# Fused attention, feed-forward and expert kernel: first pass of the first block cut after four slices, routing tables moved behind the weights, scheduler durations rewritten, load buffers pooled

## Chip, cores, metric

The kernel runs on one core of one Trainium2 chip. The metric is device time in microseconds (us) of one execution; lower is better.

## The reference

Three layers follow each other, on 3072 tokens of 384 features.

```python
for t in range(S):                                   # linear attention, 4 batches x 8 heads, head size 48
    cur = einsum('bhd,bhe->bhde', u * k[t], v[t])
    y[t] = einsum('bhd,bhde->bhe', r[t], state + cur)
    state = w * state + einsum('bhd,bhe->bhde', k[t], v[t])
h = x @ w_in                                         # 384 -> 2048
g = where(h >= 1, h, where(h <= -1, 0, (h + 1) ** 2 / 4))
x = g @ w_out                                        # 2048 -> 384
expert = argmax(normalised(x) @ normalised(emb).T / tau)   # 8 experts
out = gate * (maximum(x @ w1[expert], 0) @ w2[expert])     # 384 -> 1024 -> 384
```

All inputs are float32. The kernel keeps that precision by splitting each operand into a high and a low part and by adding three matrix products for each one of the reference (`prod3`, lines 201 to 204).

## The kernel before

**Attention** is cut into 24 units of 128 tokens. A unit loads two tiles (`att`, line 235, and `attn`, line 231). DVE scales r and k (`prep_rk`, L341); POOL makes `kk`, `ru` and `dv` (L347, L353, L355, L375) with a reduction on DVE between (`dg`, L360); PE multiplies k and r (`s0_pe`, L382); DVE masks the product (L390); PE makes the unit's output from `dv`, the carried state and the masked product (`s1_pe`, L399 to L413) and the unit's addition to the state (`s2_pe`, L422), which DVE adds and ACT decays (L433, L441). ACT and DVE split the output into `xh` and `xl` (L446, L453), which are the input of the first feed-forward layer.

**The first feed-forward layer** works on six blocks of 512 tokens, that is four units each, and on 16 slices of 128 hidden features. One slice of one block is a group of nine matrix products into `psh` (`m1_h`), a chain ACT, ACT, ACT, DVE, ACT, POOL that makes `gh` and `gl` (L529, L533, L536, L539, L543, L548), and nine products into three accumulators `acc` (`m1_out`). The weights arrive in 16 chunks, each for two slices, in turn of `w_in` and `w_out`. They are stored as 64-bit words; each chunk is one ACT, four DVE, one ACT and one POOL instruction (`w_abs`, L252; `w_bits`, L260, L262, L265, L268; `w_hi`, L283; `w_lo`, L287).

There is one set of accumulators, and so blocks can only alternate by storing a partial sum (`m1_evac`, L571 and L573, then L583 to DRAM) and by adding it later (L576). The first two blocks do that: `steps` (built from `HF`) runs slices 0 to 7 of block 0, 0 to 7 of block 1, 8 to 15 of block 0 and 8 to 15 of block 1. Blocks 2 to 5 then run their 16 slices each. The expert layer follows, with seven blocks.

**The order of the work** is made by `Schedule`, a planner in the kernel that runs at build time: every piece of work is a task with an engine, a duration, dependencies, buffers and a due time. It takes, of the tasks that can start earliest, the one due first, and the instructions are issued in that order. So each engine's queue, and SP's queue of DMAs, is fixed by the table of durations and due times. The list `T` holds the due time of each slice; `TB[m]` is the first of block m, from which the units' due times follow. Where the planner sees PE idle before the first slice, the program fills in `keep_warm` products on an unused accumulator (L460).

The routing tables (`tables3`, `tables4`, `tables5`: the normalised expert embedding and a check of w) are sixteen short DVE instructions and a few others, needed first by `pick_e0`, after the second pass of block 0. Load buffers are two for `att` and two for weight chunks (`w64`).

Of the kernel before, what the change touches and what calls it, by code (L numbers as in the profile page):

```python
# [138 lines left out]
def d_dve(n):  # L139
    return n / 960 + 0.066  # L140
# [14 lines left out]
def d_pe(n):  # L155
    return n / 2400 + 0.002
# [3 lines left out]
def fused_kernel(ctx, tc, att, wcol, wrow, ub, ucol, win, wout, emb, tau, w1, w2, out):  # L160
# [68 lines left out]
    def att_load(u, part):  # L229
# [4 lines left out]
        if part != "v":  # L234
            att_t[u] = atp.tile([128, O_K], F32, tag="att", name="att", bufs=2)
# [658 lines left out]
    for u in range(NU):  # L894
# [5 lines left out]
        ab.tag = "attb"  # L900
# [8 lines left out]
        rk = add("DVE", d_dve(1024), lambda u=u: prep_rk(u), [l0], due - 8, use=[ab])  # L909
        kk = add("Pool", d_pool(384), lambda u=u: prep_kk(u), [l2, wkc], due - 6, alloc=[kkb], use=[nb])  # L910
        ru0 = add("Pool", d_pool(384), lambda u=u: prep_ru(u, 0), [l2, ubl], due - 10, alloc=[rub], use=[nb])
        ru1 = add("Pool", d_pool(384), lambda u=u: prep_ru(u, 1), [ru0], due - 9.5, use=[nb, rub])
        dg = add("DVE", d_dve(384), lambda u=u: prep_dg(u), [ru1], due - 4.5, alloc=[dgb], use=[rub])
        dv = add("Pool", d_pool(384), lambda u=u: prep_dv(u), [dg, l1], due - 4.5, alloc=[dvb], use=[ab, dgb])
        s0 = add("PE", 1.15, lambda u=u: s0_pe(u), [rk], due - 7, alloc=[a0, a1], use=[ab])
        e0 = add("DVE", d_dve(512), lambda u=u: s0_ev(u, 0), [s0], due - 9, alloc=[atb], use=[a0])
        e1 = add("DVE", d_dve(512), lambda u=u: s0_ev(u, 1), [s0, e0], due - 9, use=[a1, atb])
        c = u % UPB
        s1 = add("PE", 2.0 if c else 1.35, lambda u=u: (xt_tiles(unit_blk[u][0]), s1_pe(u)),
# [7 lines left out]
        lo_of[u] = add("DVE", d_dve(384), lambda u=u: s3_lo(u), [s3h], due, use=[yb] + list(xbuf[m]))  # L927
        u_tasks += [lo_of[u], s1, dv, kk]
        if c != UPB - 1:
# [5 lines left out]
            p = add("DVE", 2 * d_dve(192) + 0.1, lambda u=u: s2_ev(u), [s2, s2e.get(u - 1 if c else u - 2)],  # L935
# [8 lines left out]
    for ci, c in enumerate([x for f in range(NF // 2) for x in (("in", f), ("out", f))]):  # L944
# [17 lines left out]
    for k, s in enumerate(steps):  # L962
# [6 lines left out]
        r = add("ACT", d_act(n), lambda k=k, n=n: got.update({("a", k): m1_relu(got["h", k], n)}), [h], T[k], alloc=[ab], use=[hb])  # L969
        q = add("ACT", d_act(n), lambda k=k: m1_over(got["a", k]), [r], T[k], use=[ab])  # L970
        q = add("ACT", d_act(n), lambda k=k: m1_sq(got["a", k]), [q], T[k], use=[ab])
# [373 lines left out]
```

## Time and profile before

| | |
|---|---|
| median of 3 runs | 779.70 us (778.98 to 780.13) |
| the profiled execution's own time | 779.42 us |
| its span, first to last instruction | 777.6 us |
| PE busy in the span | 745.2 us (96%) |
| DVE busy | 342.4 us (44%) |
| ACT busy | 397.4 us (51%) |
| POOL busy | 305.9 us (39%) |
| mean granted TensorE clock | 0.983 |

The span leaves 1.8 us of the execution outside. Shares over the whole span mix two stages: the first sixth, in which attention, weight chunks and slices compete, and the rest. How to read the rows below: a timeline row gives the start, the duration and the instruction, with the idle time before it in brackets; a group row gives count, busy time, mean duration in ns and idle time. A matrix product's shown duration is longer than its distance to the next one, since products are pipelined; distances are read from the starts.

### The profile page before, as it was taken

The numbers are of one execution on the slowest core, as the hardware profiler recorded it, in microseconds if no ns is written. First come the engines' busy times: TensorE is split into PE (matmuls) and PEld (weight loads), VectorE is DVE, ScalarE is ACT, GpSimd is POOL, SyncE is SP. The second block draws the span as 40 slices with busy tenths as digits, with TensorE's granted clock in tenths as the row PEclk, the third lists the DMA queues.
The fourth block names the chain that finished last, engine by engine and source line by source line (L and its number), as shares of the span: only waits on it lengthen the run. The fifth ranks groups of instructions, "written<-read, shape, count | busy, mean of one in ns | idle before, by whom it ended". The sixth has DMA issues, their size and how long they took to land.

```text
span 777.6 us, 12491 instructions
## 1 busy us (share of the span) xinstructions
PE 745.2 (96%) x5070; PEld 614.0 (79%) x5070; DVE 342.4 (44%) x584; ACT 397.4 (51%) x696; POOL 305.9 (39%) x258
## 2 busy tenths in 40 slices
PE   8878886999999999999999999999999999999996
PEld 7756665778777877887777878888798888888995
DVE  6999997721454135311452132522323333232442
ACT  3345476676346655664556645877532424242442
POOL 6877999543465255623654232333210101010000
PEclk9989989999999999999999999999999999999999
DMA  7655364210522014101212011410211111101100
GB/s 281 199 194 179 142 202 140 80 46 0 201 87 73 1 40 148 58 36 58 85 56 80 0 40 42 145 60 1 80 31 52 40 42 41 41 20 41 62 21 26
DMA packets 22277, 61.67 MB, mean 79 GB/s; under 512 B 1977, under 2 KB 7746, under 8 KB 22210
## 3 DMA queue, kind: packets, MB, share of 16 engines
q1 hardware_dynamic: 22210, 60.78, 23.0%
q8 instruction: 42, 0.69, 0.4%
q14 instruction: 25, 0.20, 0.1%
HBM read 49.76 MB, written 11.01 MB: 78 GB/s over the span
## 4 chain that ended last, share of the span: by engine, by line
PE 83%; DVE 11%; POOL 3%; issue 2%; ACT 1%; POOLq 0%; ACTq 0%; DVEq 0%
PE psh L202 13%; PE psh L203 12%; PE psh L204 12%; PE acc L202 8%; PE acc L204 8%; PE acc L203 8%; PE o L204 4%; PE o L202 4%; PE o L203 4%; PE psa L382 2%; DVE sc L265 2%; DVE sc L260 2%; DVE sc L262 1%; DVE att L341 1%; DVE at L390 1%
## 5 line engine op out<-in xcount | busy, mean ns | idle before, releaser
L548 POOL TENSOR_TENSOR gl<-a,gh 128x512 fp32r<-128x512 f32 x96 | 128.5, 1338 | 189.9 <-ACT gh L543 185.0
L539 DVE TENSOR_TENSOR a<-psh,a 128x512 f32<-128x512 f32 x96 | 66.1, 688 | 187.2 <-ACT a L536 186.9
L202 PE MATMUL psh<-xh,win_h 128*128 128x512 f32 x288 | 117.9, 409 | 8.3 <-DVE a L539 8.3
L203 PE MATMUL psh<-xl,win_h 128*128 128x512 f32 x288 | 115.8, 402 | 3.6 <-DVE xl L453 3.6
L202 PE MATMUL acc<-gh,wout_h 128*128 128x512 f32 x288 | 117.2, 407 | 2.0 <-ACT gh L543 2.0
L203 PE MATMUL acc<-gl,wout_h 128*128 128x512 f32 x288 | 115.0, 399 | 3.6 <-POOL gl L548 3.6
L529 ACT ACTIVATE a<-psh,half 128x512 f32<-128x512 f32 x96 | 65.8, 685 | 99.1 <-PE psh L204 95.8
L204 PE MATMUL psh<-xh,win_l 128*128 128x512 f32 x288 | 115.7, 402 | 0.0
L204 PE MATMUL acc<-gh,wout_l 128*128 128x512 f32 x288 | 114.7, 398 | 0.0
L543 ACT ACTIVATE gh<-a 128x512 fp32r<-128x512 f32 x96 | 60.5, 630 | 72.3 <-DVE a L539 72.1
L683 POOL TENSOR_TENSOR sq<-sq 128x512 f32<-128x512 f32 (+1 forms) x14 | 15.9, 1134 | 182.9 <-ACT sq L678 149.6
L806 ACT ACTIVATE gh<-psh 128x512 fp32r<-128x512 f32 (+1 forms) x56 | 29.9, 535 | 105.0 <-PE psh L204 98.6
L811 DVE SCALAR_TENSOR_TENSOR gl<-psh,gh 128x512 fp32r<-128x512 f32 (+1 forms) x56 | 34.3, 612 | 102.1 <-ACT gh L806 102.1
L202 PEld LDWEIGHTS psh<-xh,win_h 128*128 128x128 f32 x288 | 54.9, 190 | 24.6 <-DVE a L539 10.2
L202 PEld LDWEIGHTS acc<-gh,wout_h 128*128 128x128 f32 x288 | 54.6, 189 | 18.2 <-ACT gh L543 2.9
L203 PEld LDWEIGHTS acc<-gl,wout_h 128*128 128x128 f32 x288 | 54.7, 190 | 16.7 <-POOL gl L548 4.8
L203 PEld LDWEIGHTS psh<-xl,win_h 128*128 128x128 f32 x288 | 55.2, 192 | 16.0 <-DVE xl L453 3.9
L204 PEld LDWEIGHTS psh<-xh,win_l 128*128 128x128 f32 x288 | 55.2, 192 | 13.2
L204 PEld LDWEIGHTS acc<-gh,wout_l 128*128 128x128 f32 x288 | 54.6, 190 | 13.0
L204 PE MATMUL o<-w2h,gl 128*128 128x384 f32 x192 | 64.7, 337 | 0.0
L202 PE MATMUL o<-w2h,gh 128*128 128x384 f32 x192 | 64.7, 337 | 0.0
L203 PE MATMUL o<-w2l,gh 128*128 128x384 f32 x192 | 64.5, 336 | 0.0
(155 smaller groups left out, 1324.5 us busy)
## 6 DMA issues: line engine op xcount, KB each, us to landing
att<-att SPq DMA_DIRECT2D x22, 736.0 KB, 4.5
attn<-att SPq DMA_DIRECT2D x24, 384.0 KB, 4.2
w<-win SPq DMA_DIRECT2D x8, 768.0 KB, 4.8
w<-wout SPq DMA_DIRECT2D x8, 768.0 KB, 4.5
x1d<-x SPq DMA_DIRECT2D x6, 768.0 KB, 3.7
out<-o SPq DMA_DIRECT2D x11, 384.0 KB, 2.5
x1f<-x1d SPq DMA_DIRECT2D x5, 768.0 KB, 4.9
hw<-w SPq DMA_DIRECT2D x8, 384.0 KB, 3.8
```

The lines of the kernel that those rows point to most:

```text
L202: nc.tensor.matmul(o, lhsT=sh, rhs=mh, start=first, stop=False, skip_group_check=True)
L203: nc.tensor.matmul(o, lhsT=sh, rhs=ml, start=False, stop=False, skip_group_check=True)
L204: nc.tensor.matmul(o, lhsT=sl, rhs=mh, start=False, stop=last, skip_group_check=True)
L260: nc.vector.tensor_scalar(out=m, in0=m, scalar1=2.0 ** -15, scalar2=None, op0=ALU.max)
L265: nc.vector.scalar_tensor_tensor(out=tu, in0=hw, scalar=0xC0000000, in1=tu, op0=ALU.bitwise_and, op1=ALU.bitwise_or)
L529: nc.scalar.activation(out=a, in_=hp, func=AF.Relu, bias=half[:, 0:1], scale=0.5)
L539: nc.vector.tensor_tensor(out=a, in0=hp, in1=a, op=ALU.max)
L543: nc.scalar.activation(out=gh, in_=a, func=AF.Copy)
L548: (eng or nc.gpsimd).tensor_tensor(out=gl, in0=a, in1=gh.bitcast(F32), op=ALU.subtract)
L683: nc.gpsimd.tensor_tensor(out=q[:, 0, :n], in0=q[:, 0, :n], in1=q[:, kk, :n], op=ALU.add)
L806: nc.scalar.activation(out=gh, in_=hp, func=AF.Relu)
L811: nc.vector.scalar_tensor_tensor(out=gl, in0=hp, scalar=0.0, in1=gh.bitcast(F32), op0=ALU.max, op1=ALU.subtract)
```

## The change

- Block 0's first pass ends after slice 3 instead of 7; its second pass takes slices 4 to 15. Block 1 stays cut at 8. `steps` now comes from `parts`.
- The routing tables depend on the last weight chunk (`after=list(w_ready.values())`), and so stand behind all 16 chunks on every engine.
- The planner's durations are numbers instead of formulas of the size, and due times `T` follow a sum of DVE's work (`U_DVE` for a unit, `W_DVE` for a chunk, 0.7 for a slice); a block's first slice is set later by four times `U_PE`, and the factor 1.2 on the slices is dropped.
- The tiles `att` and `w64` share one tag of four buffers (`ld`) instead of two and two; each has 128x1536 float32 now.

No arithmetic is added or taken away. The diff, cut:

```diff
 def d_pe(n):
-    return n / 2400 + 0.002
+    return n / 2300 + 0.011
+U_DVE, U_PE, W_DVE = 4.7, 3.5, 4.8
...
-            att_t[u] = atp.tile([128, O_K], F32, tag="att", name="att", bufs=2)
+            att_t[u] = atp.tile([128, 1536], F32, tag="ld", name="att", bufs=4)
...
-        t = atp.tile([128, 768], U64, tag="w64", name="w64", bufs=2)
+        t = atp.tile([128, 1536], F32, tag="ld", name="w64", bufs=4).bitcast(U64)
...
-    HF = NF // 2
-    steps = [(m, f, 0, 512, f0, f1) for f0, f1 in ((0, HF), (HF, NF)) for m in range(2) for f in range(f0, f1)]
+    parts = ((0, 0, 4), (1, 0, 8), (0, 4, NF), (1, 8, NF))
+    steps = [(m, f, 0, 512, f0, f1) for m, f0, f1 in parts for f in range(f0, f1)]
...
-    T, t = [], 16
+    T, t, dve, seen = [], 6.0, 6.0, set()
     for m, f, c0, n, f0, f1 in steps:
+        if m not in seen:
+            dve += 4 * U_DVE
+            t = max(t, dve) if not seen else t + 4 * U_PE
+        if f % 2 == 0 and m < 2 and ("f", f) not in seen:
+            dve += 2 * W_DVE
+            t = max(t, dve - W_DVE)
+        seen |= {m, ("f", f)}
         T.append(t)
-        t += 18 * d_pe(n) * (1.2 if m < len(blocks1) - 1 else 1.0)
+        dve += 0.7
+        t += 18 * d_pe(n)
...
-        rk = add("DVE", d_dve(1024), lambda u=u: prep_rk(u), [l0], due - 8, use=[ab])
+        rk = add("DVE", 1.5, lambda u=u: prep_rk(u), [l0], due - 8, use=[ab])
...
-    due = T[HF * 3]
+    due = T[K0] - 20
...
-                 alloc=[tb[i]] if i < 2 else [], use=[])]
+                 alloc=[tb[i]] if i < 2 else [], use=[], after=list(w_ready.values()))]
```

Lines of the changed kernel stand 3 below those of the kernel before in its first half (L539 becomes L542) and 12 further on.

What it moves, at three places. On DVE, the first of the routing tables stood between two steps of the second weight chunk, beside the second unit's state. Before:

```order
L433 TENSOR_TENSOR state1_124<-pskv_295,state0_123 48x4x48 x2
L262 TENSOR_SCALAR sc_276<-sc_276 128x768
L476 TENSOR_SCALAR wrc_317<-mix_99 1x384
L477 TENSOR_TENSOR wrc_317<-wrc_317,mix_99 1x384
L478 TENSOR_REDUCE unsafe_79<-wrc_317 1x1
L479 CAST unsafe_i_82<-unsafe_79 1x1
L480 RECIPROCAL rtau_75<-rtau_75 128x1
L265 SCALAR_TENSOR_TENSOR sc_276<-w64_151,sc_276 128x768
L260 TENSOR_SCALAR sc_367<-sc_367 128x768
```

Now they follow the last step of the sixteenth chunk, L271:

```order
L271 SCALAR_TENSOR_TENSOR sc_1584<-w64_1332,sc_1584 128x768
L479 TENSOR_SCALAR wrc_1672<-mix_99 1x384
L480 TENSOR_TENSOR wrc_1672<-wrc_1672,mix_99 1x384
L481 TENSOR_REDUCE unsafe_79<-wrc_1672 1x1
L482 CAST unsafe_i_82<-unsafe_79 1x1
L483 RECIPROCAL rtau_75<-rtau_75 128x1
L487 TENSOR_TENSOR esq_1689<-mix_99 8x384
```

All sixteen instructions went that way; the rows around them closed up.

On DVE, at the end of block 0's first pass, where the partial sum is copied out of accumulator 1. Before, the copy (L571) follows the tenth max (L539), amid chunk 13:

```order
L265 SCALAR_TENSOR_TENSOR sc_1189<-w64_1131,sc_1189 128x768
L539 TENSOR_TENSOR a_1220<-psh_1193,a_1220 128x512
L268 SCALAR_TENSOR_TENSOR sc_1189<-w64_1131,sc_1189 128x768
L360 TENSOR_REDUCE dg_1283<-ru_1241 128x8
L260 TENSOR_SCALAR sc_1267<-sc_1267 128x768
L262 TENSOR_SCALAR sc_1267<-sc_1267 128x768
L265 SCALAR_TENSOR_TENSOR sc_1267<-w64_1185,sc_1267 128x768
L539 TENSOR_TENSOR a_1263<-psh_1223,a_1263 128x512
L268 SCALAR_TENSOR_TENSOR sc_1267<-w64_1185,sc_1267 128x768
L571 COPY x1_1322<-acc1_743 128x512
```

Now the copy (L574) follows the last output of the eighth unit (L456), amid chunk 7, with four max instructions ahead of it:

```order
L271 SCALAR_TENSOR_TENSOR sc_850<-w64_809,sc_850 128x768
L263 TENSOR_SCALAR sc_945<-sc_945 128x768
L265 TENSOR_SCALAR sc_945<-sc_945 128x768
L456 TENSOR_TENSOR xl_657<-psy_972,xh_656 128x3x128
L268 SCALAR_TENSOR_TENSOR sc_945<-w64_880,sc_945 128x768
L363 TENSOR_REDUCE dg_1032<-ru_968 128x8
L574 COPY x1_1030<-acc1_740 128x512
L271 SCALAR_TENSOR_TENSOR sc_945<-w64_880,sc_945 128x768
L363 TENSOR_REDUCE dg_1061<-ru_1036 128x8
L542 TENSOR_TENSOR a_1048<-psh_1020,a_1048 128x512
```

The copy and the blocks' switch stand six chunks earlier in the queue, and behind the outputs of the same eight units.

On PE, at the start of block 5, whose first slice is `psh_4469` before and `psh_4500` now. Before, it follows the products of block 4's fifteenth slice:

```order
L204 MATMUL acc1_3842<-gh_4428,wout_l_92 128x512
L202 MATMUL acc2_3843<-gh_4428,wout_h_91 128x512
L203 MATMUL acc2_3843<-gl_4430,wout_h_91 128x512
L204 MATMUL acc2_3843<-gh_4428,wout_l_92 128x512
L202 MATMUL psh_4469<-xh_3876,win_h_89 128x512
L203 MATMUL psh_4469<-xl_3877,win_h_89 128x512
L204 MATMUL psh_4469<-xh_3876,win_l_90 128x512
```

Now it follows the output step of the block's own last unit (L402 to L416):

```order
L402 MATMUL psy_4461<-ident_70,dv_4339 128x128 x3
L406 MATMUL psy_4461<-att_3783,state1_124 32x128 x8
L409 MATMUL psy_4461<-att_3783,state1_124 32x128 x4
L412 MATMUL psy_4461<-at_4458,att_3783 32x128 x8
L416 MATMUL psy_4461<-at_4458,att_3783 32x128 x8
L205 MATMUL psh_4500<-xh_3871,win_h_89 128x512
L206 MATMUL psh_4500<-xl_3872,win_h_89 128x512
L207 MATMUL psh_4500<-xh_3871,win_l_90 128x512
```

Before, the output step of that unit stood 18 products further ahead, with block 4's last slice and one accumulation between; now the slice that reads it comes next. At the starts of blocks 2, 3 and 4 the last unit's step moved towards the slice too, with one other group of products left between.

## Rows read from the trace of the kernel before

**Rows 1.** The page, part 2: busy tenths of PE and DVE in 40 slices of the span

```profile
PE   8878886999999999999999999999999999999996
DVE  6999997721454135311452132522323333232442
```

**Rows 2.** Busy time by stretch, 135 to 260 us: stretch, span, then each engine (instructions), clock, DMA

```profile
135.00:260.00 125.00, 125.00 (x811) 99.48 (x810) 52.18 (x80) 73.96 (x127) 60.50 (x51) 1.00 0.23 79
```

**Rows 3.** Groups on DVE, 0 to 131 us: line, shapes, count | busy us, mean ns | idle

```profile
L341 DVE TENSOR_TENSOR att<-att,pwt 128x1024 f32<-128x1024 f32 x10 | 19.7, 1968 | 0.0
L265 DVE SCALAR_TENSOR_TENSOR sc<-w,sc 128x768 uint32<-128x768 uint32 x13 | 17.7, 1364 | 0.2
L268 DVE SCALAR_TENSOR_TENSOR sc<-w,sc 128x768 uint32<-128x768 uint32 x13 | 14.9, 1145 | 0.1
L260 DVE TENSOR_SCALAR sc<-sc 128x768 f32<-128x768 f32 x13 | 14.8, 1140 | 3.4 <-ACT sc L252 3.4
L262 DVE TENSOR_SCALAR sc<-sc 128x768 uint32<-128x768 uint32 x13 | 14.5, 1117 | 0.1
...
L539 DVE TENSOR_TENSOR a<-psh,a 128x512 f32<-128x512 f32 x11 | 7.5, 680 | 0.1
```

**Rows 4.** Busy time of DVE in the four stretches that hold the routing tables, summed

```profile
sum 7.82, DVE 7.50; mean DVE 1.87
```

**Rows 5.** Timeline of DVE at the eighth unit: start us, us, instruction

```profile
109.43 0.55 DVE L453 TENSOR_TENSOR xl<-psy,xh 128x384 fp32r<-128x384 f32 x1
```

**Rows 6.** Timeline of PE at the first slice

```profile
48.88 0.79 PE L203 MATMUL psh<-xl,win_h 128*128 128x512 f32 x1 [3.57 <-DVE xl L453]
49.47 0.63 PE L204 MATMUL psh<-xh,win_l 128*128 128x512 f32 x1
49.90 0.63 PE L202 MATMUL psh<-xh,win_h 128*128 128x512 f32 x1
```

**Rows 7.** Timeline of PE at the thirteenth slice

```profile
135.03 0.39 PE L202 MATMUL psh<-xh,win_h 128*128 128x512 f32 x1
135.26 0.39 PE L203 MATMUL psh<-xl,win_h 128*128 128x512 f32 x1
```

**Rows 8.** Timeline of attention steps on PE

```profile
114.85 0.57 PE L422 MATMUL pskv<-att,kk 128*48 128x48 f32 x16
...
123.64 1.16 PE L382 MATMUL psa<-att 64*128 64x128 f32 x16
```

**Rows 9.** Groups on POOL, 0 to 131 us

```profile
L355 POOL TENSOR_TENSOR ru<-ru,attn 128x384 f32<-128x384 f32 x12 | 17.1, 1425 | 0.6
L548 POOL TENSOR_TENSOR gl<-a,gh 128x512 fp32r<-128x512 f32 x10 | 16.6, 1659 | 8.1 <-ACT gh L543 8.1
...
L287 POOL TENSOR_TENSOR wout_l<-sc,wout_h 128x768 fp32r<-128x768 f32 x6 | 14.0, 2337 | 0.3 <-ACT wout_h L283 0.3
```

**Rows 10.** Timeline of POOL and DVE around 69 us

```profile
68.21 1.87 POOL L548 TENSOR_TENSOR gl<-a,gh 128x512 fp32r<-128x512 f32 x1 [0.48 <-ACT gh L543]
...
68.86 2.31 DVE L341 TENSOR_TENSOR att<-att,pwt 128x1024 f32<-128x1024 f32 x1
```

**Rows 11.** Group of the same DVE line, 135 to 560 us

```profile
L341 DVE TENSOR_TENSOR att<-att,pwt 128x1024 f32<-128x1024 f32 x14 | 17.4, 1244 | 23.9 <-DMA att<-att 23.8
```

**Rows 12.** Timeline of a late slice and unit on PE, POOL and DVE

```profile
475.86 0.39 PE L204 MATMUL psh<-xh,win_l 128*128 128x512 f32 x1
...
478.19 0.49 PE L399 MATMUL psy<-ident,dv 128*128 128x128 f32 x3
478.47 0.69 DVE L539 TENSOR_TENSOR a<-psh,a 128x512 f32<-128x512 f32 x1 [3.20 <-ACT a L536]
...
479.73 0.62 PE L413 MATMUL psy<-at,att 128*32 128x128 f32 x16
479.90 1.28 POOL L548 TENSOR_TENSOR gl<-a,gh 128x512 fp32r<-128x512 f32 x1 [4.20 <-ACT gh L543]
...
480.94 0.56 DVE L453 TENSOR_TENSOR xl<-psy,xh 128x384 fp32r<-128x384 f32 x1 [1.77 <-ACT xh L446]
```

More of the change, by code (lines that the diff above doesn't have):

```diff
@@ L899, in fused_kernel @@
         ab, rub, dgb, dvb, atb, kkb = [Buf(x) for x in ("att", "ru", "dg", "dv", "at", "kk")]
-        ab.tag = "attb"
+        ab.tag = "ld"
         a0, a1, yb = [Buf("att") for _ in range(3)]
@@ L926, in fused_kernel @@
             xhu[u] = s1
-        lo_of[u] = add("DVE", d_dve(384), lambda u=u: s3_lo(u), [s3h], due, use=[yb] + list(xbuf[m]))
+        lo_of[u] = add("DVE", 0.56, lambda u=u: s3_lo(u), [s3h], due, use=[yb] + list(xbuf[m]))
         u_tasks += [lo_of[u], s1, dv, kk]
@@ L934, in fused_kernel @@
             s2pe[u] = s2
-            p = add("DVE", 2 * d_dve(192) + 0.1, lambda u=u: s2_ev(u), [s2, s2e.get(u - 1 if c else u - 2)],
+            p = add("DVE", 0.75, lambda u=u: s2_ev(u), [s2, s2e.get(u - 1 if c else u - 2)],
                     due - 2.5, alloc=[state_b[u]], use=[kvb] + ([state_b[u - 1]] if c else []))
@@ L947, in fused_kernel @@
         due = T[k] - 6 + (4 if kind == "out" else 0)
-        wb, sb = Buf("w64"), Buf("x1")
+        wb, sb = Buf("ld"), Buf("x1")
         wl = add("SP", 2.19, lambda c=c: w_load(c), due=first.get(f"w{ci}", due - 10 - 2), alloc=[wb])
-        p = add("ACT", d_act(768), lambda c=c: w_abs(c), [wl], due - 8, alloc=[sb], use=[wb])
+        p = add("ACT", 0.9, lambda c=c: w_abs(c), [wl], due - 8, alloc=[sb], use=[wb])
         for i in range(4):
-            p = add("DVE", d_dve(768) if i > 1 else d_fast(768), lambda c=c, i=i: w_bits(c, i), [p], due - 6 + i * 0.8,
+            p = add("DVE", (1.06, 1.1, 1.35, 1.1)[i], lambda c=c, i=i: w_bits(c, i), [p], due - 6 + i * 0.8,
                     use=[sb] + ([wb] if i > 1 else []))
-        p = add("ACT", d_act(768), lambda c=c: w_hi(c), [p], due - 2, use=[sb])
-        p = add("Pool", d_pool(768), lambda c=c: w_lo(c, nc.gpsimd), [p], due, use=[sb])
+        p = add("ACT", 0.84, lambda c=c: w_hi(c), [p], due - 2, use=[sb])
+        p = add("Pool", 2.1, lambda c=c: w_lo(c, nc.gpsimd), [p], due, use=[sb])
         w_ready[c] = p
@@ L968, in fused_kernel @@
         prev_h = h_of[k] = h
[L969 to L973 removed]
+        r = add("ACT", 0.65, lambda k=k, n=n: got.update({("a", k): m1_relu(got["h", k], n)}), [h], T[k], alloc=[ab], use=[hb])
+        q = add("ACT", 0.65, lambda k=k: m1_over(got["a", k]), [r], T[k], use=[ab])
+        q = add("ACT", 0.65, lambda k=k: m1_sq(got["a", k]), [q], T[k], use=[ab])
+        q = add("DVE", 0.7, lambda k=k: m1_max(got["a", k], got["h", k]), [q], T[k], use=[ab, hb])
+        q = add("ACT", 0.65, lambda k=k, n=n: got.update({("gh", k): m1_gh(got["a", k], n)}), [q], T[k], alloc=[ghb], use=[ab])
         def gl(k=k, s=s):
             gq[s[:3]] = got["gh", k], m1_gl(got["a", k], got["gh", k], s[3])
[L977 removed]
+        q = add("Pool", 1.35, gl, [q], T[k], alloc=[glb], use=[ab, ghb])
         key = (m, f0)
@@ L1028, in fused_kernel @@
     xb, key = pick_x
-    due = T[HF * 3] + 20
+    due = T[K0] + 6
     pe0 = add("PE", 0.3, lambda: got.update(lp=pick_e0(x1_tiles[key], t3["ef"])), pick_dep + [t5], due, alloc=[pb], use=[xb])
```

22 lines of the change are left out of this document (10 added, 12 removed).

## The prediction

> **What bounds the kernel now.** I read the busy shares over time first. PE is below 90% only in the first seven of 40 slices of time, 19.4 us each, and DVE is at 90% or more in the second to the sixth of these and hardly half busy behind them [rows 1]. The stretches say the same: from 135 us on PE has no idle time at all [rows 2]. So the end is fixed by how soon PE gets through the products of that first stretch, and DVE is the queue that is full there. The groups of DVE show with what: 13 weight chunks of four instructions, 1.14 + 1.12 + 1.36 + 1.15 = 4.77 us each, ten scalings of units at 1.97 us [rows 3], and 7.8 us of routing tables that nobody needs before the second pass [rows 4]. The first slice starts at 48.9 us, and PE had waited 3.57 us for the unit's `xl` [rows 6]. The thirteenth slice starts at 135.03 us [rows 7]; behind it PE never waits [rows 1, 2].
>
> So I count from two marks: the eighth unit's `xl`, which ends at 109.43 + 0.55 = 109.98 us [rows 5] and after which block 1 can start, and the thirteenth slice.
>
> **First term: what DVE no longer does ahead of the eighth unit.** The two orders, counted up to that `xl`, differ by this much: four first steps (1.140), four second (1.117), five third (1.364) and four fourth (1.145) of chunks, 4.56 + 4.47 + 6.82 + 4.58 = 20.43 us; three max instructions of slices at 0.68, 2.04; one scaling of a ninth unit, 1.97 [rows 3]; and the sixteen table instructions, 7.82 [rows 4]. Masks, states and outputs are equal in number, and of the unit's reduction, a short one, there is one less, which I leave out. Together 32.3 us, so DVE alone would have the eighth `xl` at 109.98 - 32.3 = 77.7 us. That keeps the idle time that DVE had in that stretch and takes today's durations, waits included.
>
> PE is nearly as late. Its first slice moves up only by what left DVE ahead of it, half of the tables, 3.9 us [rows 4], to 45. Up to the eighth unit it then has four slices and four accumulations, which are eight groups of nine products at 0.23 us [rows 7], 16.9; three first steps of units at 1.16 [rows 8], 3.5; four output steps of 479.73 + 0.62 - 478.19 = 2.2 us at most [rows 12], 8.5; three state steps at 0.57 [rows 8], 1.7. That is 75.6 us with no wait and at the full clock. After its wait of 3.57 us the clock was at the lower level, with products 0.43 us apart instead of 0.23 [rows 6, 7]; two such stretches of eleven products cost 4.4. With both queues that close, neither can absorb the other's waits: I take 81 us for the first slice of block 1, between 77.7 and 87 (75.6, two slow stretches, two more waits of 3.57).
>
> **Second term: from there to the thirteenth slice.** In both orders eight slices and six accumulations, of slices 5 to 10, lie between the fifth slice's start and the thirteenth's: 14 x 9 x 0.233 = 29.4 us. DVE's order has six, five, six and six steps of chunks and nine max up to the thirteenth max: 6.8 + 5.6 + 8.2 + 6.9 + 6.1 = 33.6 us, of which 27.5 in steps [rows 3]. PE's way to the same point is 29.4, one slice of 2.1 and 2.9 us from a slice's last product to the end of its max [rows 12], 34.4: level. POOL has no less. Up to the twelfth `gl` it has seven `ru` or `kk` at up to 1.43, six `w_lo` at 2.34 and eight `gl` at 1.66: 10.0 + 14.0 + 13.3 = 37.3 us [rows 9], against 29.4 us to the thirteenth slice and 33.6 to the fifteenth, behind which that `gl` is read. PE's lead of two to three slices hides part of it. I take 5 us of stalls, between 0 and 8.
>
> **Third term: work that the marks move.** At the thirteenth slice two first steps of units 9 and 10 and one state step are done before, and not yet after the change: 2 x 1.16 + 0.57 = 2.9 us [rows 8] that PE does later.
>
> **Fourth term: the starts of blocks 2 to 5.** The due times set these blocks' last units close to the slice that reads them. A unit's output takes from the end of L413 to the end of `xl` 481.50 - 480.35 = 1.2 us; a slice needs from its last product to `gl` 481.18 - 476.25 = 4.9 us [rows 12]. At blocks 2, 3 and 4 a group of 1.16 us or 2.1 us lies between unit and slice and covers most of the first; at block 5 nothing does, and its third slice is issued before its first accumulation, where only two `psh` buffers exist: the max of the first ends 2.9 us after its products, 0.8 later than the second slice's 2.1. So 1.2 + 0.8 there and some 0.3 at each of the others: 3 us, between 0 and 10.
>
> **At nothing** I cost the tables' new place: from the sixteenth chunk on DVE is half idle, as it is today [rows 2]. Likewise the shared load buffers: no bytes change, and the third unit's load now waits for the first chunk's last step, which stands seven instructions ahead of the scaling that the load feeds. If that cover fails, it is the fourth rival.
>
> **Sum**, made against the profiled execution (span 777.6, own time 779.4, which is 0.3 under the median): what remains from the thirteenth slice is 777.6 - 135.0 = 642.6. Then 642.6 + 81 + 29.4 + 5 + 2.9 + 3 = 763.9, and 1.8 outside the span: **766 us**, 1.7% faster.
>
> **Rivals.**
> 1. Everything is covered: eighth unit at 77.7, no stalls, no cost at block starts: 642.6 + 77.7 + 29.4 + 2.9 + 1.8 = 754 us. For it: DVE carries that count alone. Against: POOL's 37 us.
> 2. POOL and DVE shut each other out. At 68.21 a `gl` lasts 1.87 us and the scaling that starts inside it at 68.86 lasts 2.31 [rows 10]; the same scaling takes 1.24 in the later stage [rows 11] and 1.97 in this one [rows 3]. If their two-operand instructions share one door, the earlier stage is limited by their sum, and packing chunks and slices closer only lengthens each. Price, at a tenth more on the chunk steps alone: of the 7, 7, 6 and 6 steps ahead of the eighth `xl`, 30.9 us [rows 3], 3.1; of the 27.5 us of steps up to the thirteenth max, 2.8; of some 18 us behind it, 1.8: 766 + 7.7 = 774 us. The Trainium skill, "SBUF — State Buffer", section "Who interferes with whom", states just this: VectorE and GpSimd share a pair of ports under an exclusive lock, and a VectorE instruction with two SBUF inputs keeps out a GpSimd one that reads SBUF for its whole length. By that rule the lengthening in the rows is waiting, the trace agrees, and this rival's time would be the forecast.
> 3. **Slower.** PE drains at each of four block starts. The lag between a slice and its accumulation, three slices today, shrinks to one there, so any late ACT or POOL instruction is exposed. Price of one drain: 1.2 + 4.9 us idle and then eleven products 0.2 us slower each, 8.3 us. Four of them instead of the 3 us above: 766 - 3 + 33 = 796 us. It decides from about (13.4 + 3) / 4 = 4 us a start on. Against it: two or more groups of other products still lie ahead of each in its queue.
> 4. The shared buffers undo the gain: an early load waits for the slower user of its buffer, in one queue. If each of some 14 loads ahead of the eighth unit came 1 us later than DVE asks, the 13.7 us would be gone: 780 us, no change. Against it: today's order waits for buffers just so.
>
> **Chances.** Forecast 0.55 (758 to 770), first rival 0.15, second 0.19, third 0.07, fourth 0.04. The range must hold the forecast, most of the first rival and the second: 756 to 777; it leaves out the rest of the first, the third and the fourth. A measurement can tell some 0.2%, 1.6 us, from no change; so faster 0.89, same 0.04 (the fourth), slower 0.07 (the third).
>
> **What would show it.** In the changed profile PE's share should reach 90% for good near 85 us instead of 135, the eighth `xl` should end between 77 and 85 us, with no table instruction on DVE ahead of it, and the first slice should start near 45. The thirteenth slice should start at 111 to 119. Waits of PE behind it should add up to under 5 us and lie at block starts. The prediction is wrong if the eighth `xl` comes after 90 us, if PE waits for POOL's `gl` for more than 8 us, or if the granted clock falls behind 135 us.

## The result, and the profile after

The changed kernel takes **771.99 us** (median of 4 runs, 770.07 to 774.81) against 779.91 of the kernel before on the same chip: ratio 0.9895, 95% interval 0.9872 to 0.9917. Predicted were 766, between 756 and 777, with 758 to 770 for the forecast alone. The profiled execution took 772.31 us, with a span of 770.6 us.

The page, part 2, of the changed kernel answers to [rows 1]; a slice of time is 19.3 us:

```profile
PE   8998998999999999999999999999999999999996
DVE  7989897883464115511261122531332323332332
```

PE is at 90% from the second slice to the last but one, but for two dips, in the fourth (58 to 77 us) and in the seventh (116 to 135 us); DVE is no longer full anywhere for long. The marks on PE's timeline, the first, the fifth and the thirteenth slice, answer to [rows 6, 7]:

```profile
43.07 0.48 PE L205 MATMUL psh<-xh,win_h 128*128 128x512 f32 x1
...
76.26 0.49 PE L205 MATMUL psh<-xh,win_h 128*128 128x512 f32 x1 [0.61 <-ACT xh L449]
77.99 0.50 PE L206 MATMUL psh<-xl,win_h 128*128 128x512 f32 x1 [1.24 <-DVE xl L456]
...
111.64 0.40 PE L205 MATMUL psh<-xh,win_h 128*128 128x512 f32 x1
```

The first product of the fifth slice reads `xh` alone and starts at 76.26; the wait of 1.24 us at 77.99 is for the eighth unit's `xl`, which stands on DVE's timeline here, 32.0 us sooner than in [rows 5]:

```profile
77.39 0.54 DVE L456 TENSOR_TENSOR xl<-psy,xh 128x384 fp32r<-128x384 f32 x1
```

So block 1 starts 4.7 us sooner than I had taken (81), or 3.0 by the product that reads `xl`; the thirteenth slice starts 23.4 us sooner than before (135.03) and 3.8 sooner than I had summed (115.4). But the end came only 7.0 us sooner in the span. Behind the thirteenth slice PE used to have no idle time; now these are its longest waits there, with the idle time in brackets:

```profile
124.90 0.50 PE L205 MATMUL psh<-xh,win_h 128*128 128x512 f32 x1 [2.06 <-DVE a L542]
167.07 0.50 PE L205 MATMUL psh<-xh,win_h 128*128 128x512 f32 x1 [1.81 <-DVE a L542]
225.88 0.50 PE L206 MATMUL psh<-xl,win_h 128*128 128x512 f32 x1 [1.02 <-DVE xl L456]
303.01 0.56 PE L425 MATMUL pskv<-att,kk 128*48 128x48 f32 x16 [0.78 <-DVE at L393]
386.84 0.56 PE L425 MATMUL pskv<-att,kk 128*48 128x48 f32 x16 [0.78 <-DVE at L393]
483.22 0.50 PE L205 MATMUL psh<-xh,win_h 128*128 128x512 f32 x1 [2.46 <-DVE a L542]
```

They lie in three places. At 124.90 PE waits for a max that stands behind two chunk steps (rows at the end of this section). At 167.07 it waits for a max that stands behind the routing tables; the timeline of POOL and DVE there shows their first instruction, which lasts 1.98 us (0.44 before the change), and, behind six more, the max that PE waits for:

```profile
161.95 1.83 POOL L290 TENSOR_TENSOR wout_l<-sc,wout_h 128x768 fp32r<-128x768 f32 x1
162.01 1.98 DVE L479 TENSOR_SCALAR wrc<-mix 1x384 f32<-1x384 f32 x1 [2.17 <-POOL gl L551]
...
166.35 0.67 DVE L542 TENSOR_TENSOR a<-psh,a 128x512 f32<-128x512 f32 x1
```

The tables take one of the buffers `a` of the slices, which is free when a `gl` is done: so DVE idled 2.17 us with the max queued behind. After PE's wait the clock fell for some 3 us: PE's busy time by stretch shows 38.19 us of 40 and a mean clock of 0.96, where before it had 40.00 and 1.00:

```profile
160.00:200.00 40.00, 38.19 (x247) 29.45 (x246) 20.63 (x45) 20.44 (x35) 17.24 (x16) 0.96 0.27 88
```

The other four rows are the starts of blocks 2 to 5. Last, the groups of DVE that answer to [rows 3], the four steps of a chunk, first up to 78 us and then from 78.5 to 131:

```profile
L268 DVE SCALAR_TENSOR_TENSOR sc<-w,sc 128x768 uint32<-128x768 uint32 x7 | 10.1, 1445 | 0.0
L271 DVE SCALAR_TENSOR_TENSOR sc<-w,sc 128x768 uint32<-128x768 uint32 x6 | 8.2, 1360 | 0.0
L265 DVE TENSOR_SCALAR sc<-sc 128x768 uint32<-128x768 uint32 x7 | 6.5, 936 | 0.1
L263 DVE TENSOR_SCALAR sc<-sc 128x768 f32<-128x768 f32 x7 | 6.4, 917 | 2.7 <-ACT sc L255 2.5
```

```profile
L268 DVE SCALAR_TENSOR_TENSOR sc<-w,sc 128x768 uint32<-128x768 uint32 x7 | 12.2, 1749 | 0.1
L265 DVE TENSOR_SCALAR sc<-sc 128x768 uint32<-128x768 uint32 x6 | 11.0, 1838 | 0.1
L271 DVE SCALAR_TENSOR_TENSOR sc<-w,sc 128x768 uint32<-128x768 uint32 x7 | 9.1, 1295 | 0.1
L263 DVE TENSOR_SCALAR sc<-sc 128x768 f32<-128x768 f32 x6 | 5.7, 949 | 0.1
```

The mean durations of the four steps add up to 4.66 us ahead of block 1 and to 5.83 behind its start, though the instructions are the same. The trace of before has 4.77 over both stretches, and 4.58 and 4.97 in the two apart. DVE's and POOL's timeline around 120 us shows the difference: L263 takes 0.55 us with POOL idle; the step that starts beside POOL's `w_lo` of 1.85 takes 2.23, where 936 ns were its mean up to 78 us, and the next one, beside a `gl`, 1.92. Behind them stands the max that PE waits for at 124.90:

```profile
119.00 0.55 DVE L263 TENSOR_SCALAR sc<-sc 128x768 f32<-128x768 f32 x1
...
120.03 1.85 POOL L290 TENSOR_TENSOR wout_l<-sc,wout_h 128x768 fp32r<-128x768 f32 x1 [1.77 <-ACT wout_h L286]
120.07 2.23 DVE L265 TENSOR_SCALAR sc<-sc 128x768 uint32<-128x768 uint32 x1
...
121.83 1.59 POOL L551 TENSOR_TENSOR gl<-a,gh 128x512 fp32r<-128x512 f32 x1
...
122.33 1.92 DVE L268 SCALAR_TENSOR_TENSOR sc<-w,sc 128x768 uint32<-128x768 uint32 x1
...
124.17 0.68 DVE L542 TENSOR_TENSOR a<-psh,a 128x512 f32<-128x512 f32 x1
```

### The profile page after: what moved, and what is told of

It is laid out like the page before. It is cut to its first block, busy times and chain, and to the rows that moved or that the text cites. A ratio compares the mean times of both kernels' runs of the same rounds, so it can differ in the third digit from the quotient of the medians.

```text
span 770.6 us, 12607 instructions
## 1 busy us (share of the span) xinstructions
PE 744.9 (97%) x5118; PEld 614.6 (80%) x5118; DVE 345.2 (45%) x584; ACT 396.8 (51%) x696; POOL 299.3 (39%) x258
## 4 chain that ended last, share of the span: by engine, by line
PE 75%; POOL 8%; DVE 6%; issue 4%; DMA 3%; ACT 2%; SPq 0%; DVEq 0%; POOLq 0%; ACTq 0%
PE psh L205 11%; PE psh L206 11%; PE psh L207 11%; PE acc L205 7%; PE acc L206 7%; PE acc L207 7%; PE o L207 4%; PE o L205 4%; PE o L206 4%; POOL gl L551 2%; PE psa L385 2%; DMA att<-att 2%; POOL dv L378 2%; POOL ru L356 1%; POOL ru L358 1%
## 5 line engine op out<-in xcount | busy, mean ns | idle before, releaser
L551 POOL TENSOR_TENSOR gl<-a,gh 128x512 fp32r<-128x512 f32 x96 | 132.6, 1382 | 193.5 <-ACT gh L546 193.5
L542 DVE TENSOR_TENSOR a<-psh,a 128x512 f32<-128x512 f32 x96 | 66.1, 689 | 191.7 <-ACT a L539 191.3
L206 PE MATMUL psh<-xl,win_h 128*128 128x512 f32 x288 | 115.4, 401 | 2.7 <-DVE xl L456 2.6
L814 DVE SCALAR_TENSOR_TENSOR gl<-psh,gh 128x512 fp32r<-128x512 f32 (+1 forms) x56 | 34.4, 614 | 97.3 <-ACT gh L809 97.3
L206 PEld LDWEIGHTS acc<-gl,wout_h 128*128 128x128 f32 x288 | 54.3, 189 | 15.6 <-POOL gl L551 3.8
```

The source lines that it names most:

```text
L206: nc.tensor.matmul(o, lhsT=sh, rhs=ml, start=False, stop=False, skip_group_check=True)
L542: nc.vector.tensor_tensor(out=a, in0=hp, in1=a, op=ALU.max)
L551: (eng or nc.gpsimd).tensor_tensor(out=gl, in0=a, in1=gh.bitcast(F32), op=ALU.subtract)
L814: nc.vector.scalar_tensor_tensor(out=gl, in0=hp, scalar=0.0, in1=gh.bitcast(F32), op0=ALU.max, op1=ALU.subtract)
```

## The experiments

Three questions were put: which part of the change carries the gain, where the missing 6 us went, and what POOL and DVE take from each other. All kernels beside each other; the slices' starts and the span are of the profiled execution, the ratio is to the kernel before:

| kernel | slice 1 | 5 | 13 | span | median us | ratio, 95% interval |
|---|---|---|---|---|---|---|
| before | 44.8 | 76.7 | 135.0 | 777.6 | 779.9 | |
| the change | 43.1 | 76.3 | 111.6 | 770.6 | 772.0 | 0.9895 (0.9872 to 0.9917) |
| cut at 8 and 8 again | 44.3 | 62.1 | 116.5 | 788.7 | 787.6 | 1.0093 (1.0066 to 1.0121) |
| cut alone | 61.4 | 100.7 | 140.8 | 787.4 | 789.2 | 1.0124 (1.0107 to 1.0142) |
| tables in front | 48.2 | 83.3 | 119.6 | 780.6 | 781.1 | 1.0014 (0.9994 to 1.0033) |
| buffers 2 and 2 | 44.5 | 81.7 | 116.0 | 774.7 | 777.8 | 0.9971 (0.9957 to 0.9985) |
| PE not filled | 47.1 | 79.5 | 115.8 | 772.6 | 773.6 | 0.9916 (0.9887 to 0.9946) |
| units 14 us earlier | 42.8 | 76.1 | 112.3 | 764.3 | 766.2 | 0.9823 (0.9806 to 0.9839) |
| tables in a load buffer | 43.2 | 76.5 | 111.8 | 764.9 | 766.9 | 0.9838 (0.9821 to 0.9854) |
| both of these | 43.2 | 76.4 | 111.7 | 760.0 | 761.8 | 0.9773 (0.9757 to 0.9790) |
| both, 22 us earlier | 42.6 | 75.8 | 111.7 | 761.2 | 762.1 | 0.9769 (0.9753 to 0.9786) |
| both, `w_lo` on DVE | 43.9 | 78.4 | 111.8 | 758.1 | 759.1 | 0.9731 (0.9715 to 0.9747) |
| both, `w_lo` twice | 51.1 | 89.7 | 131.3 | 784.3 | 786.9 | 1.0104 (1.0083 to 1.0125) |
| both, `w_lo` split | 42.5 | 75.7 | 111.0 | 757.2 | 759.4 | 0.9733 (0.9720 to 0.9747) |

(In the kernels cut at 8 and 8 the fifth slice still belongs to block 0.)

### What carries the gain

**The cut undone**, all else as changed:

```diff
-    parts = ((0, 0, 4), (1, 0, 8), (0, 4, NF), (1, 8, NF))
+    parts = ((0, 0, 8), (1, 0, 8), (0, 8, NF), (1, 8, NF))
```

> The changed kernel with the first passes of blocks 0 and 1 cut at 8 and 8 again; everything else of the change stays. Theory A (the split carries the gain, since at 8 and 8 PE needs eight chunks instead of six ahead of block 1 and DVE is the full queue): the eighth unit's xl ends later than 78 us, and the time is 776 to 779 us, most of the 8 us gone. Theory B (the rewritten durations and due times carry it, by a better order and by products that keep the clock up): 771 to 773 us, as the changed kernel.

787.6 us: the loss was expected, its size was not. The thirteenth slice starts at 116.45, 18.6 us sooner than in the kernel before, and all of that and more goes again behind it. PE's longest wait, the last row, is for a max that stands behind the tables, as in the changed kernel; the tables wait here for the second of two `gl` of 2.1 us each (POOL, DVE and PE):

```profile
151.07 4.23 POOL L551 TENSOR_TENSOR gl<-a,gh 128x512 fp32r<-128x512 f32 x2
...
155.33 1.94 DVE L479 TENSOR_SCALAR wrc<-mix 1x384 f32<-1x384 f32 x1 [1.18 <-POOL gl L551]
...
160.94 0.79 PE L205 MATMUL psh<-xh,win_h 128*128 128x512 f32 x1 [6.22 <-DVE a L542]
```

From 200 to 480 us it is idle for another 8.2. I have not followed the rest of the loss.

**The cut alone**, in the kernel before, with its tables, durations, due times and buffers:

```diff
-    steps = [(m, f, 0, 512, f0, f1) for f0, f1 in ((0, HF), (HF, NF)) for m in range(2) for f in range(f0, f1)]
+    parts = ((0, 0, 4), (1, 0, 8), (0, 4, NF), (1, 8, NF))
+    steps = [(m, f, 0, 512, f0, f1) for m, f0, f1 in parts for f in range(f0, f1)]
...
```

The part left out is bookkeeping at build time: `s3_lo` keeps a finished unit's entries in the program's own lists.

> The kernel before with only the first two blocks cut at slices 4 and 8; tables, due times, durations and buffers as before. Theory (the split is what moves block 1 forward, the rest keeps it from being spoilt): the split alone leaves the tables among the chunks and due times that ask for block 1's units too late, so it gains less than the whole change: 772 to 778 us, with the fifth slice 5 us or more later than the changed kernel's 76.3. Rival A (the split is everything): 768 to 773 us. Rival B (without new due times the split gains nothing): 778 to 785 us.

789.2 us, slower than before, beyond even the second rival. The first slice starts at 61.35 instead of 44.84. On PE's timeline a product of the tables stands ahead of it, before which PE sat idle for 4.26 us, and then a whole unit's output:

```profile
54.15 0.48 PE L497 MATMUL pset<-ident,mix 8*128 8x8 f32 x3 [4.26 <-DVE at L390]
...
56.00 0.85 PE L399 MATMUL psy<-ident,dv 128*128 128x128 f32 x3
```

That unit is the fifth, block 1's first. By the old formulas a slice is 18 x (512/2400 + 0.002) x 1.2 = 4.65 us, so with four slices ahead of it block 1 is due at 16 + 18.6 = 34.6 and its first unit at 34.6 - 6 - 22.2 = 6.4; block 0's last unit is due at 16 - 6 = 10. The planner was asked for the fifth unit before the fourth. In the changed kernel T puts them at 34.8 and 23.6. That the due times are what the cut lacks is argued from the formulas and the order; no run has the cut with the new due times and nothing else. What the two runs show is that the cut without the rest is 1.2% slower than before, the rest without the cut 0.9% slower, and both 1% faster.

**The tables in front again:**

```diff
-                 alloc=[tb[i]] if i < 2 else [], use=[], after=list(w_ready.values()))]
+                 alloc=[tb[i]] if i < 2 else [], use=[])]
```

> The changed kernel without the tables' dependency on the last weight chunk, so that the planner puts them early again. Theory A (DVE is the full queue up to the eighth unit, and each table instruction there delays block 1): up to 7.8 us later at the eighth unit, less the 3.5 us that the tables cost in their late place (1.8 us of wait at 167 us and nine products at half clock): 774 to 777 us. Theory B (DVE's queue has slack that the tables only fill, while their late place costs 3.5 us): 768 to 770 us.

781.1 us: no different from the kernel before, so without the tables' new place the whole gain is gone, 9 us, some 4 more than my theory's upper end. All of it is there at the thirteenth slice (119.64, 8.0 later); the remainder is the same within 2.0 (661.0 and 659.0). The stretches of the tables in [rows 4] are 7.82 us long, with DVE busy for 7.50. One of them shows how a small instruction costs more than it holds: on DVE the subtraction of 24 columns takes 1.27 us beside POOL's `w_lo` (0.83 in the changed kernel, 0.18 in the one below with earlier units), the max waits behind it, and PE for that max:

```profile
89.08 1.80 POOL L290 TENSOR_TENSOR win_l<-sc,win_h 128x768 fp32r<-128x768 f32 x1
...
89.64 1.27 DVE L516 TENSOR_TENSOR enx<-ef,enx 128x24 fp32r<-128x24 f32 x1
90.84 0.68 DVE L542 TENSOR_TENSOR a<-psh,a 128x512 f32<-128x512 f32 x1
...
91.57 0.50 PE L205 MATMUL psh<-xh,win_h 128*128 128x512 f32 x1 [3.77 <-DVE a L542]
```

**Load buffers two and two again:**

```diff
-            att_t[u] = atp.tile([128, 1536], F32, tag="ld", name="att", bufs=4)
+            att_t[u] = atp.tile([128, O_K], F32, tag="att", name="att", bufs=2)
...
-        t = atp.tile([128, 1536], F32, tag="ld", name="w64", bufs=4).bitcast(U64)
+        t = atp.tile([128, 768], U64, tag="w64", name="w64", bufs=2)
...
```

The rest of the edit tells the planner of the two pools.

> The changed kernel with two load buffers for attention tiles and two for weight chunks, as before, and the planner told so. Theory A (the shared buffers move no time): 771 to 773 us. Theory B (the fourth buffer lets chunks be loaded earlier between units, which the order of the first 80 us needs): 774 to 777 us.

777.8 us, just above Theory B's range: the shared buffers are worth 5.8. The waits of SP's queue up to 82 us (total us, times, longest) show what changes. In the changed kernel, and with two and two, L240 (the load of a unit) and L249 (of a chunk):

```profile
SPq L249 <- PE psy L416: 15.7, 5, 6.0
SPq L240 <- DVE sc L271: 13.3, 3, 5.6
SPq L249 <- DVE sc L271: 10.7, 2, 6.1
...
SPq L240 <- PE psy L416: 1.2, 2, 1.0
```

```profile
SPq L240 <- PE psy L416: 26.7, 6, 7.7
...
SPq L249 <- DVE sc L271: 15.6, 6, 5.7
```

With two buffers of their own the units' loads (L240) wait six times for an earlier unit's output, 26.7 us in all; with four shared they wait 14.5 us in all, 13.3 of them for chunks. The chunks' loads (L249) wait the longer, 26.4 us instead of 15.6. So the waits don't get fewer, they move from the units to the chunks. The scaling of the eighth unit then comes sooner, first with two and two, then in the changed kernel (DVE):

```profile
66.03 1.39 DVE L344 TENSOR_TENSOR att<-att,pwt 128x1024 f32<-128x1024 f32 x1
```

```profile
55.65 1.93 DVE L344 TENSOR_TENSOR att<-att,pwt 128x1024 f32<-128x1024 f32 x1 [0.80 <-DMA att<-att]
```

The eighth `xl` ends at 81.64 with two and two, 3.7 us later than in the changed kernel. That the units' earlier loads are the reason is read from these rows; no run has them alone.

**PE not filled.** In the changed kernel the planner's gaps ahead of the first slice are filled with more `keep_warm` products than before (190 in the trace instead of 142), and PE's clock was at its upper level from the start, where before it had fallen several times. Without the filling:

```diff
-                keep_warm(max(0, int((task.start - end - 0.1) / 0.22)))
+                pass
```

> The changed kernel without the products that only keep PE busy before the first slice (the nine at the very start stay). Theory A (the new order's greater number of them is why the clock stayed at its higher level from 10 to 78 us, where the kernel before fell to the lower one three times): the clock is at the lower level in parts of the first 80 us, the first block's slices are 0.43 us per product instead of 0.23, and the time is 775 to 780 us. Theory B (DVE sets the pace up to the eighth unit, whatever PE's clock): the clock falls, but the eighth unit's xl moves by under 2 us and the time is 772 to 774 us.

773.6 us, 1.6 more, but the two intervals overlap: what the filling is worth in the whole isn't shown. The time is Theory B's, its mark is not: the eighth `xl` ends at 81.21, 3.3 us later. The clock of the first 40 us (third column from the end) falls to 0.79, where it is 1.00 with the filling, and the fifth slice is 3.3 us later too; about half of that is made good by the end.

```profile
0.00:40.00 40.00, 23.45 (x303) 18.96 (x303) 31.14 (x52) 10.72 (x22) 30.25 (x34) 0.79 0.67 244
```

### Where the missing time went

**Units of blocks 2 to 5 due 14 us earlier:**

```diff
-        due = TB[m] - 6 - (3 - i) * 7.4
+        due = TB[m] - 6 - (3 - i) * 7.4 - (14 if m > 1 else 0)
```

> The changed kernel with the units of blocks 2 to 5 due 14 us earlier. Theory: PE's waits at the starts of these four blocks, some 7 us in the changed kernel, come from units that end just ahead of the slice that reads them; earlier units take away most of it: 766 to 769 us, with under 2 us of idle PE at the starts of blocks 3, 4 and 5. Rival: the waits come from the chain of the slices (max, square, gl) whatever the units do, or the units, asked for earlier, only crowd the stage with the chunks: 771 to 775 us.

766.2 us, 5.8 less: the theory. PE's busy time from 200 to 480 us, in the changed kernel and in this one:

```profile
200.00:480.00 280.00, 275.39 (x2190) 219.02 (x2189) 92.90 (x147) 154.72 (x275) 115.37 (x110) 1.00 0.18 59
```

```profile
200.00:480.00 280.00, 279.50 (x2122) 222.21 (x2122) 97.51 (x149) 162.09 (x286) 115.08 (x107) 1.00 0.17 55
```

4.6 us of idle time became 0.5, and the 2.46 us at block 5 went too.

**The tables in a load buffer** instead of in buffers `a`:

```diff
-    tb = [Buf("a") for _ in range(3)]
+    tb = Buf("ld")
...
-            wrc = tmp512("wrc")[32:33, 0:DM]
+            r["tab"] = atp.tile([128, 1536], F32, tag="ld", name="tab", bufs=4)
+            wrc = r["tab"][32:33, 0:DM]
...
```

> The changed kernel with the tables' scratch in one load buffer instead of in the slices' buffers a. Theory: the tables cost 3.5 us behind the sixteenth chunk because they wait for a gl to give up its buffer, with the next max behind them in DVE's queue; without that wait the idle time of PE near 167 us goes: 768 to 770 us. Rival: the place behind the weights is at fault, DVE's queue is held by seven short instructions and by a POOL instruction beside them whichever buffer they write: 771 to 773 us.

766.9 us, 5.1 less, more than the theory had. But the edit did more than I meant: short of a free load buffer, the planner put the tables at 400 us. So this run shows what the tables cost behind the sixteenth chunk, the 3.5 us read from the rows, and beside it the stall at block 5 is gone too (0.22 us there instead of 2.46). It does not tell the wait for the buffer from the place in DVE's queue; that stays open.

**Both**, and **both with 22 us** instead of 14:

> Both edits, units of blocks 2 to 5 due 14 us earlier and the tables in a load buffer. If the two losses are separate, their gains add: 763 to 768 us. Rival: moving the units fills the place that the tables need, and the sum is no better than the better of the two alone: 767 to 772 us.

> Units of blocks 2 to 5 due 22 us earlier instead of 14. Theory: 14 us took nearly all of PE's waits at the block starts, so 8 us more bring nothing: 760 to 763 us. Rival: the third block's units now fall into the stage with the last chunks and the second pass and make it stall: 764 us or more.

761.8 us, just below the range: the gains add (5.8 and 5.1 alone, 10.2 together). The stall at block 5 went in either run alone and can be gained once only; PE's wait of 2.06 us near 124 us became 0.97 with both, which makes up for part of it. Eight us more bring nothing (762.1), as the theory said.

### What POOL and DVE take from each other

Three versions of the kernel with both edits. **`w_lo` on DVE**, **twice on POOL**, and **on POOL for six chunks, then on DVE**:

```diff
-        p = add("Pool", 2.1, lambda c=c: w_lo(c, nc.gpsimd), [p], due, use=[sb])
+        p = add("DVE", 1.0, lambda c=c: w_lo(c, nc.vector), [p], due, use=[sb])
```

```diff
-        eng.tensor_tensor(out=l, in0=m, in1=h.bitcast(F32), op=ALU.subtract)
+        for _ in range(2):
+            eng.tensor_tensor(out=l, in0=m, in1=h.bitcast(F32), op=ALU.subtract)
```

```diff
-        p = add("Pool", 2.1, lambda c=c: w_lo(c, nc.gpsimd), [p], due, use=[sb])
+        p = add(*(("Pool", 2.1) if ci < 6 else ("DVE", 1.2)),
+                lambda c=c, ci=ci: w_lo(c, nc.gpsimd if ci < 6 else nc.vector), [p], due, use=[sb])
```

> The kernel with early units and tables in a load buffer, with the low part of each weight chunk computed by DVE instead of POOL. Theory (DVE and POOL wait for each other): POOL gives up 16 instructions of 1.9 to 2.1 us, DVE takes on 16 of about 0.96 us (what a subtraction of 768 elements lasts on DVE in the later stage), and the four chunk steps, 5.07 us on average in the kernel without the move, get shorter by about as much as POOL's instruction had held them up: chunk steps at 4.6 us or less, fifth slice at 73 to 77 us, 756 to 762 us. Rival (each engine has its own limit, and DVE's is the tighter one): chunk steps stay at 5.0 us or more, DVE has 0.96 us more for each of six chunks ahead of the eighth unit, fifth slice at 80 to 83 us, 765 to 770 us.

> The same kernel with POOL computing the low part of each chunk twice. Theory (DVE and POOL wait for each other): DVE's four chunk steps rise from 5.07 us on average to 5.6 or more and the scaling of a unit from 1.54 us, though not one of DVE's instructions has changed, while instructions with an operand from PSUM (max 0.68 us) keep their length; 769 us or more. Rival (they don't): DVE's steps stay within 0.15 us of 5.07, and only what follows POOL's queue is late: 764 to 769 us.

> The kernel with early units and tables in a load buffer, with the low part of chunks 1 to 6 on POOL and of chunks 7 to 16 on DVE. With all sixteen on DVE the fifth slice starts 2.0 us later (78.4 against 76.4) and the seventeenth 3.2 us sooner (127.2 against 130.3). Theory (what counts ahead of block 1 is DVE's queue, behind it the two engines' sum): each half keeps its better place, fifth slice at 76 to 77 us, seventeenth at 125 to 127 us, 756 to 758.5 us. Rival (the second gain was got only because the late start had let POOL and DVE catch up): fifth slice as early, seventeenth at 128 us or later, 759 to 762 us.

On DVE: 759.1 us. The groups of DVE from 0 to 150 us, first in the kernel with both edits, then with `w_lo` on DVE:

```profile
L268 DVE SCALAR_TENSOR_TENSOR sc<-w,sc 128x768 uint32<-128x768 uint32 x15 | 22.7, 1516 | 0.2
L271 DVE SCALAR_TENSOR_TENSOR sc<-w,sc 128x768 uint32<-128x768 uint32 x15 | 20.3, 1354 | 0.1
L265 DVE TENSOR_SCALAR sc<-sc 128x768 uint32<-128x768 uint32 x15 | 18.1, 1206 | 0.2
...
L263 DVE TENSOR_SCALAR sc<-sc 128x768 f32<-128x768 f32 x15 | 14.8, 991 | 1.6 <-ACT sc L255 1.4
```

```profile
L268 DVE SCALAR_TENSOR_TENSOR sc<-w,sc 128x768 uint32<-128x768 uint32 x14 | 17.7, 1266 | 0.1
L271 DVE SCALAR_TENSOR_TENSOR sc<-w,sc 128x768 uint32<-128x768 uint32 x14 | 14.8, 1058 | 0.0
...
L265 DVE TENSOR_SCALAR sc<-sc 128x768 uint32<-128x768 uint32 x15 | 13.8, 920 | 0.2
L263 DVE TENSOR_SCALAR sc<-sc 128x768 f32<-128x768 f32 x15 | 13.4, 891 | 4.5 <-ACT sc L255 4.5
...
L290 DVE TENSOR_TENSOR win_l<-sc,win_h 128x768 fp32r<-128x768 f32 x7 | 9.6, 1369 | 1.2 <-ACT win_h L286 1.1
```

The four steps fall from 5.07 to 4.13 us, as far as the theory asked, though DVE's instructions are the same. `w_lo`, DVE's fifth instruction now, takes 1.34 on average, so a chunk costs DVE 0.4 more than before the move and POOL about 2.0 less. The fifth slice was later than expected (78.4), the end in the middle of the theory's range: 2.7 us below the kernel without the move, and the two intervals don't meet. These 2.7 us are not the price of the waiting between DVE and POOL alone: POOL's queue is also shorter by some 2 us a chunk. From its fifth to its seventeenth slice this kernel took 48.8 us instead of 53.9. PE's waits there for a `gl` (1.16 us) and for two max (0.28 and 0.97) were gone, the clock, at 0.95 from 76 to 112 us in the kernel without the move, stayed at 1.00, and one other wait for a max grew from 0.74 to 1.74.

Twice on POOL: 786.9 us, the theory's side, but DVE's steps rose only to 1.02 + 1.14 + 1.67 + 1.54 = 5.37, half of what I asked and more than the rival allowed; the max kept its 0.68, and the scaling rose from 1.54 to 1.65. What broke was POOL's queue. POOL was full from 40 to 80 us already without the doubling (38.89 of 40 us busy, now 39.15), and what stands in its queue comes later: PE waited for `gl` up to 2.71 us at a time (up to 1.16 before), and the eighth `xl` ended at 90.21 instead of 78.04, with DVE busy for 31.4 of these 40 us instead of 36.8. So more POOL work hurt here by POOL's own queue more than through the length of DVE's instructions.

Split: 759.4 us, the rival's time. The marks came as the theory said (fifth slice 75.7, seventeenth 126.5), but the lead of 2.65 us over the version with all on DVE is 0.66 at the seventeenth slice. What takes the lead away in between was not followed. I count the two versions as equal, and both beat the changed kernel by 1.6%.

## Why the prediction was right, and where it was not

The time lay in the range, and the kernel became faster as forecast, but by 8 us instead of 14: 772 is outside the forecast's own 758 to 770 and nearest to the second rival's 774. In spans, 763.9 was the sum and 770.6 the result: -4.7 at the fifth slice, +1.0 from there to the thirteenth, +10.5 behind it (659.0 against 642.6 + 2.9 + 3). PE's waits account for nearly all of the 10.5: 4.0 more than summed at the block starts, 3.5 at the tables (half of it products at the lower clock behind the wait), 2.3 at 116 and 124.90, 0.55 at 752.97.

- **First term, right in its count, 4.7 us too long in its allowance.** DVE alone was to have the eighth `xl` at 77.7; it ended at 77.93. That this agrees to 0.2 us is partly luck: the count of instructions is the trace's, but DVE's instructions up to that `xl` add up to 36.4 us less than before, not 32.3 (the eight scalings took 1.49 us each instead of 1.97), and its idle time, which the count kept as it was, grew by about as much as that error. I had added two stretches at the lower clock and waits. PE's waits from the first slice to the fifth were a few tenths each, and the clock did not fall before 79 us. The run without filling shows what held it: with the clock down, the fifth slice came at 79.5. One slip of reading: the row at 48.88 [rows 6] is the first slice's second product; its first had started at 44.84. The first, which reads `xh` alone, moved by 1.8 us to 43.07, the second, which had waited for `xl`, by 5.5 to 43.39; the sum let the slice gain 3.9.
- **Second term, right in size, by luck in what it is made of:** 35.4 us against 34.4. Beyond the 29.4 us of products I had taken 5 us of stalls, from POOL's count in [rows 9]; they came to 6.0. Some 1.5 of them are the wait for block 1's own `xl` at 77.99, 1.5 the eight products behind it that ran 0.43 us apart instead of 0.23 (mean granted clock 0.72 from 78 to 84 us), 0.9 a wait for a max at 84.51, and only 1.4 a wait for POOL's `gl` at 109.67. So POOL's count did not set the pace.
- **Third term:** its counts stand in the traces (up to the thirteenth slice PE had done two first steps of units and one state step more before than after); its 2.9 us were not separately measured.
- **Fourth term, mis-sized:** 3 us for the block starts, measured 7.0 (1.02 at block 2, 1.38 at block 3, 1.50 at block 4, 3.07 at block 5). The mechanism was the one named, a unit that ends just ahead of its slice: due 14 us earlier, all but 0.5 us is gone. At block 5 the place was named too, the third slice waiting for the max of the first; 0.8 us were summed for it and 2.46 measured. What I did not see there was ACT's queue, where the first weights of the expert layer (L638 at 480.67, which waited 0.56 us for their load) stood between two steps of the slice's chain, and DVE's, where their low part (L642 at 481.60) stood ahead of the max.
- **Tables at nothing: failed.** I asked whether DVE had time there, and it had (20.6 us busy of 40). The cost was in the queue: a buffer that a `gl` must give up, seven instructions ahead of a max, and PE two slices behind. 3.5 us by the rows.
- **Not in the sum:** 2.3 us at 116 and 124.90, with the chunks that now run beside slices. Waits behind the thirteenth slice were to stay under 5 us and at block starts; they were 11.1 us, 4.2 of them elsewhere (not counting the 0.55 in the expert layer).
- **One sign of being wrong did appear:** the granted clock was not to fall behind 135 us, and after the wait for the tables it did (0.76 from 165 to 172 us). PE's share was to reach 90% for good near 85 us; it dipped once more, from 116 to 135. Both are the terms that were left out or put at nothing.
- **Shared buffers at nothing: failed to the other side.** They are worth 5.8 us. I compared the loads' order and the bytes, and not whom each load waits for. The fourth rival feared the reverse.
- **The second rival was nearest in time (774) and true as a mechanism.** A tenth on the chunk steps was its price. Against the same stretches of the trace before, they hardly grew up to 78 us (4.66 us against 4.58) and grew by 17% from 78.5 to 131 (5.83 against 4.97). There it reached PE: ahead of the max at 124.17 stood two steps of 2.23 and 1.92 us, where the shortest of their lines in the same run take 0.55 and 0.94, and PE waited 2.06. How much of the 6 us above the forecast is this rival's, no run tells. Taking `w_lo` off POOL gave 2.7 us, POOL's shorter queue included; the share of `gl`, `ru` and `kk` was not tried.
- **The third rival** fell: no block start drained PE for more than 3.1 us. **The first** had the eighth unit right (77.7) and everything behind it wrong.
- What the prediction did not weigh at all is that its parts hold each other up. Cut, tables and buffers are worth 15.6, 9.1 and 5.8 us taken out one by one, 30.5 in all, where the change gives 8.

## What to carry to other kernels

A new order of work and the due times that a planner derives it from are one change: try neither alone, and look for the unit that is asked for before its turn. Before a piece of work is costed at nothing because its engine is half idle, look at what stands behind it in that engine's queue, whose buffer it takes, and who releases it. And when the last input of a stage is planned just in time, more lead (14 us here) cost nothing and gave back 6.

## What was not expected of the hardware

The length of a DVE instruction in the stage with POOL at work says little about its size. One row of 384 elements took 1.98 us (L479) beside a `w_lo` and 0.44 in the kernel before; 24 columns took 1.27, 0.83 and 0.18 in three kernels; L263 ranged from 0.55 to 2.33 us in the changed kernel, on the same shape. Instructions with an operand from PSUM, the max (0.67 to 0.69) and the mask (0.68), kept their length beside the same POOL instructions. The Trainium skill, "SBUF — State Buffer", section "Who interferes with whom", has the rule: the two engines share a port pair, whoever comes first holds it for its whole instruction, and a VectorE instruction with at most one SBUF input outside the two-port modes stays clear of it. The rows here agree, 1.98 us for 384 elements beside a POOL instruction of 1.83 above all. What the waiting cost the whole kernel, no row tells; `w_lo` on DVE gave 2.7 us, in which POOL's shorter queue and the clock have a share.
